# One fused attention and mixture-of-experts kernel, rewritten: stages ordered by a planner in the source, score blocks turned by VectorE, shares multiplied in by GpSimd, two experts per sum matmul

## The chip, the core and the metric

The kernel runs on one NeuronCore of a Trainium2 chip. The metric is the device time of one execution in microseconds (us). Engines are named as in the profile: PE is TensorE (matmuls; PEld its weight loads), DVE is VectorE, ACT is ScalarE, POOL is GpSimd, SP is SyncE, which here only issues DMAs. Everything is float32, or float32r for the largest matmuls.

## What is computed

Three layers follow each other, without a round trip to memory between them:

```
# 1: attention through 32 memory slots; B=4, H=8, S=576, head 64
a = softmax(phi over s);  k_m = a^T k;  v_m = a^T v          # (b,h,32,64)
x = softmax(q k_m^T / 8) v_m                                 # (2304, 512)
# 2: four experts, every token through each, weighted by its shares p
x = sum_e p[:, e] * (relu(x @ w1[e]) @ w2[e])                # F = 1024
# 3: eight experts on 32 slots (4 each)
logits = x @ phi2                                            # (2304, 32)
slots  = softmax(logits over tokens)^T @ x
out    = softmax(logits over slots) @ [relu(slots_e @ v1[e]) @ v2[e]]
```

## The kernel before

Layer 2 is never multiplied out for all tokens. `logits` needs only `h @ (w2[e] @ phi2)`, so a small matrix M = w2·phi2 is made once (`m_stages`, chunks of 512 rows: PE transposes L471, matmuls L485, fold L495). `slots` needs only the sums over tokens of token weight × share × h, which are multiplied by w2 at the very end. Layer 1 is folded too: the attention weights A stay unmultiplied, and v_m is multiplied into w1 instead, chunk by chunk (`g_mult`, L384; `g_out` splits the result G into a high and a low float32r half, L394 and L395).

The tokens go through in five **units**: the whole batches 0, 1 and 2 (two ranges of 288 tokens each), then the two halves of batch 3. A unit has 8 chunks n (expert n // 2, half of its 1024 hidden columns) of 4 blocks. One **up** (`up`, L425 to L427) is one block for one range: six float32r matmuls of 128 by 288 (high by high, high by low, low by high, for two halves of the contraction) into a PSUM bank of the pool `psm` (2 banks). ACT takes it out with the relu into hT (L431); once both ranges are there, DVE transposes hT in 32 by 32 blocks into `hid` (L433), so that tokens lie on partitions. There are 256 ups. After each chunk `logits` (L448) multiplies hT by M.

After each expert `expert` transposes the logits (L526) and multiplies by the expert's shares and adds up, on POOL for experts 0 to 2 (L532 to L535). After a unit, `group` follows: `whole` (PE, L543) gathers the logits, `stats` takes a running maximum and the exponentials (L551 to L571), `weights` makes `we` = weight × share, one slice per expert, expert 0 on POOL and 1 to 3 on DVE (L585), and `sums` (L596) multiplies `we` into `hid`: per block of 32 tokens and expert, four matmuls of 32 by 32 by 256 columns, one per 32 partitions, into four banks.

The attention of batch b+1 is made between the ups of batch b: `kv_stages` (maxima, exponentials, k_m, v_m) and, per tile of 128 queries, `q_stages`: four transposes of q (L287), scores with queries on the partitions (L300), softmax on DVE and ACT (L305 to L320), two PE transposes of the result (L328) and the split into A's halves (L333, L334). Five tiles make a batch; the last has 64 queries.

All orders are written out by hand: each engine runs its instructions in the order in which the source emits them (`manual_schedule`), and `pump` emits one background item after each block of ups. All DMAs go through SP's queue in the source's order. At the end, 160 blocks of 256 KB of w2, v1 and v2 stream through whatever buffers have come free (`fill`, `fetch`, `done`), from the start of the last unit on but for six; at the very end `combine` (L969, copies L976 and L978) writes the output in two column halves through a pool of 5 buffers.

One float32 matmul appears as two instructions in the profile, one float32r matmul as one; a transpose is one.

Of the kernel before, what the change touches and what calls it, by code (L numbers as in the profile page):

```python
# [1 line left out]

# [13 lines left out]
@with_exitstack  # L16
def kernel(
    ctx: ExitStack,
    tc: tile.TileContext,
    q: bass.AP,  # L20
    k: bass.AP,
    v: bass.AP,
    phi: bass.AP,
    dprob: bass.AP,
    w1: bass.AP,
    w2: bass.AP,
    phi2: bass.AP,
    v1: bass.AP,
    v2: bass.AP,
    out: bass.AP,  # L30
):
# [4 lines left out]

    nc = tc.nc
# [4 lines left out]
    FH = 512  # L46
# [3 lines left out]

    const = ctx.enter_context(tc.tile_pool(name="const", bufs=1))
    att = ctx.enter_context(tc.tile_pool(name="att", bufs=1))
    pc = ctx.enter_context(tc.tile_pool(name="pc", bufs=1))
    hTp = ctx.enter_context(tc.tile_pool(name="hTp", bufs=5))
    rawp = ctx.enter_context(tc.tile_pool(name="rawp", bufs=2))
    gp = ctx.enter_context(tc.tile_pool(name="gp", bufs=2))
    bigp = ctx.enter_context(tc.tile_pool(name="bigp", bufs=5))
    psm = ctx.enter_context(tc.tile_pool(name="psm", bufs=2, space=bass.MemoryType.PSUM))
    psl = ctx.enter_context(tc.tile_pool(name="psl", bufs=2, space=bass.MemoryType.PSUM))
    psa = ctx.enter_context(tc.tile_pool(name="psa", bufs=4, space=bass.MemoryType.PSUM))  # L60

    def bank():
        return psa.tile([128, 512], F32, tag="at", name="at")

    def mbank():
        return psm.tile([128, 512], F32, tag="mm", name="mm")

    def big(shape, name, dt=F32):
        return bigp.tile(shape, dt, tag="big", name=name)

    ident = const.tile([128, 128], F32)
    si = const.tile([128, 32], F32)
    rr = const.tile([128, 4, 32], F32)
    r2 = const.tile([128, 4, 32], F32)
    ind = const.tile([128, 3], F32)
    phi2_sb = const.tile([128, 4, NSLOT], F32)
    dp = const.tile([128, 18, E], F32)
    dps = const.tile([128, 18], F32)
    pe = const.tile([128, B, NT, E], F32)
    ct = const.tile([128, S], F32)  # L80
    A = [const.tile([128, 2, 2, S], F32R, tag=f"A{n}", name=f"A{n}") for n in range(2)]
    kbd = [const.tile([128, 4, 2, NM], F32, name=f"kbd{n}") for n in range(2)]
    vb = [const.tile([128, 128], F32, name=f"vb{n}") for n in range(2)]
    M = const.tile([128, 4 * NCH, NSLOT], F32)
    srun = const.tile([128, 8, 4, 32], F32)
    mrun = const.tile([128, 1], F32)
    zrun = const.tile([128, 1], F32)


    ph_t, kv_t, q_t = {}, {}, {}  # L90


    def load_phi(b):

        t = att.tile([128, 36, NM], F32, tag="ph", name="ph")
        src = phi[b].rearrange("(i c) s m -> c i s m", c=2)
        for c in range(2):
            nc.sync.dma_start(
                out=t[:, 16 * c:16 * c + 16, :].rearrange("p (i r) m -> p i (r m)", i=4),
                in_=src[c, :, 0:512, :].rearrange("i (p r) m -> p i (r m)", r=4),  # L100
            )
        for c in range(2):
            nc.sync.dma_start(
                out=t[64 * c:64 * c + 64, 32:36, :],
                in_=src[c, :, 512:576, :].rearrange("i p m -> p i m"),
            )
        ph_t[b] = t

    def load_kv(b, w):

        src = (k, v)[w][b].rearrange("(i c) s d -> c i s d", c=2)
        if w == 0:
            kv_t[b, "t"] = att.tile([128, 2, 4, HD], F32, tag="kt", name="kt")
            kv_t[b] = big([128, 2, 2, 4, 4 * HD], "kv")
        for c in range(2):
            nc.sync.dma_start(
                out=kv_t[b, "t"][64 * c:64 * c + 64, w],
                in_=src[c, :, 512:576, :].rearrange("i p d -> p i d"),
            )
        for c in range(2):  # L120
            nc.sync.dma_start(
                out=kv_t[b][:, w, c],
                in_=src[c, :, 0:512, :].rearrange("i (p r) d -> p i (r d)", r=4),
            )

    def load_q(b, ti):

        t = att.tile([128, H, HD], F32, tag="q", bufs=2, name="q")
        if ti < 4:
            nc.sync.dma_start(  # L130
                out=t, in_=q[b, :, 0:512, :].rearrange("h (p r) d -> r p h d", r=4)[ti]
            )
# [225 lines left out]
    def load_w1(s):  # L358
# [708 lines left out]
```

## Time and profile before

| | |
|---|---|
| time, median of 3 runs | 687.84 us (687.55, 687.84, 690.6) |
| span of the profiled execution | 690.1 us |
| busy share of the span, PE / DVE / ACT / POOL | 83% / 45% / 29% / 5% |
| chain that ended last, share by engine | PE 55%, DVE 17%, DMA 11%, ACT 7%, issue 6% |
| DMA in total | 106.22 MB, mean 154 GB/s |

The time of the profiled execution is not marked; only the run of 690.6 us is longer than the span of 690.1 us, so it stands at 690.6, with 0.5 us around the span. A busy PE is not PE at its peak: matmuls are pipelined, and the clock that was granted to PE moved between 1.2 and 2.4 GHz. "PEclk" gives it as a share of 2.4 GHz, as a mean over a stretch.

### The profile page before, as it was taken

How to read it: one execution, taken by the hardware profiler on the slowest of the kernel's cores; microseconds unless marked ns; L12 is line 12 of the kernel's file. 1: busy time of each engine (PE TensorE's matmuls, PEld its weight loads, DVE VectorE, ACT ScalarE, POOL GpSimd, SP SyncE). 2: the span in 40 equal slices, each digit the busy share in tenths (PEclk: the TensorE clock that was granted, in tenths of full speed). 3: DMA queues.
4: the chain of work that ended last, by engine and by line, in shares of the span. 5: the costliest groups of instructions: out<-in, count | busy, mean ns of one | idle time of the engine just before them, and what ended most of it. 6: DMA issues, size and time to landing. Idle time of an engine off the chain costs nothing.

```text
span 690.1 us, 15584 instructions
## 1 busy us (share of the span) xinstructions
PE 571.0 (83%) x6750; PEld 396.3 (57%) x6750; DVE 310.0 (45%) x663; ACT 196.8 (29%) x478; POOL 35.3 (5%) x39
## 2 busy tenths in 40 slices
PE   7688988788868889797789898867896996897885
PEld 6566775566646667565556776644555884332232
DVE  5665444533360854645356466444445453121012
ACT  2334332333330434333123334311333141010012
POOL 0000001001010001010100101010010010000000
PEclk9989998899979999979899999989998898899995
DMA  8858431333110763113047241511310497899995
GB/s 203 288 151 256 163 108 53 123 123 123 62 62 4 211 175 101 62 62 123 3 126 202 77 144 47 169 63 63 120 65 0 159 331 261 277 376 350 347 337 188
DMA packets 96867, 106.22 MB, mean 154 GB/s; under 512 B 30752, under 2 KB 64032, under 8 KB 96800
## 3 DMA queue, kind: packets, MB, share of 16 engines
q1 hardware_dynamic: 96800, 105.24, 48.1%
q8 instruction: 53, 0.87, 0.5%
q14 instruction: 14, 0.11, 0.1%
HBM read 100.50 MB, written 4.72 MB: 152 GB/s over the span
## 4 chain that ended last, share of the span: by engine, by line
PE 55%; DVE 17%; DMA 11%; ACT 7%; issue 6%; SPq 2%; POOL 1%; ACTq 0%; DVEq 0%; POOLq 0%
PE mm L425 10%; PE at L596 9%; PE mm L427 8%; DMA v<-in_moe_w_dram 8%; PE mm L426 7%; PE lb L448 6%; PE at L384 4%; DVE g L395 3%; DVE h L433 3%; ACT hT L431 3%; PE at L495 1%; PE mm L882 1%; DMA out_dram<-ot 1%; PE at L471 1%; PE at L485 1%
## 5 line engine op out<-in xcount | busy, mean ns | idle before, releaser
L425 PE MATMUL mm<-A,g 128*128 128x288 f32 x512 | 174.7, 341 | 13.7 <-ACT hT L431 12.7
L431 ACT ACTIVATE hT<-mm 128x288 f32<-128x288 f32 x256 | 104.2, 412 | 264.6 <-PE mm L427 264.1
L433 DVE STREAM_TRANSPOSE h<-hT 128x576 f32<-128x576 f32 (+1 forms) x160 | 104.4, 654 | 156.0 <-ACT hT L431 155.5
L427 PE MATMUL mm<-A,g 128*128 128x288 f32 x512 | 158.3, 309 | 7.7 <-DVE g L395 7.3
L426 PE MATMUL mm<-A,g 128*128 128x288 f32 x512 | 157.0, 307 | 0.0
L425 PEld LDWEIGHTS mm<-A,g 128*128 128x128 f32 x512 | 101.8, 199 | 67.7 <-ACT hT L431 33.4
L427 PEld LDWEIGHTS mm<-A,g 128*128 128x128 f32 x512 | 101.9, 199 | 11.2 <-DVE g L395 10.5
L426 PEld LDWEIGHTS mm<-A,g 128*128 128x128 f32 x512 | 102.6, 200 | 0.4
L596 PE MATMUL at<-h,we 32*32 32x256 f32 x2304 | 60.0, 449 | 25.4 <-POOL we L585 15.4
L596 PEld LDWEIGHTS at<-h,we 32*32 32x32 f32 x2304 | 41.6, 112 | 43.2 <-POOL we L585 17.0
L395 DVE TENSOR_TENSOR g<-at,g 128x512 fp32r<-128x512 f32 x64 | 42.7, 670 | 9.4 <-ACT g L394 9.4
L448 PE MATMUL lb<-hT,M 128*32 128x288 f32 x512 | 45.2, 460 | 0.0
L1021 PE MATMUL mm<-v,hz 128*8 128x256 f32 x256 | 34.8, 380 | 6.4 <-DMA v<-in_moe_w_dram 3.5
L384 PE MATMUL at<-raw,vb 64*32 64x512 f32 x512 | 38.9, 627 | 0.1
L394 ACT CAST g<-at 128x512 fp32r<-128x512 f32 x64 | 37.2, 582 | 0.2 <-PE at L384 0.2
L605 DVE SCALAR_TENSOR_TENSOR srun<-srun,fo,at 128x256 f32<-128x256 f32 x16 | 6.6, 475 | 47.3 <-PE at L596 47.3
L976 DVE COPY ot<-at 128x512 f32<-128x512 f32 x8 | 5.4, 690 | 48.4 <-PE at L969 36.2
L1021 PEld LDWEIGHTS mm<-v,hz 128*8 128x8 f32 x256 | 8.6, 87 | 30.8 <-DMA v<-in_moe_w_dram 20.0
L300 PE MATMUL at<-kbd,qt 128*128 128x64 f32 (+1 forms) x160 | 19.3, 264 | 5.9 <-ACT qt L291 5.3
L311 ACT ACTIVATE ex<-ex 128x256 f32<-128x256 f32 (+1 forms) x20 | 8.3, 417 | 51.6 <-DVE ex L307 51.6
L300 PEld LDWEIGHTS at<-kbd,qt 128*128 128x128 f32 (+1 forms) x160 | 17.8, 180 | 8.0 <-ACT qt L291 6.9
L448 PEld LDWEIGHTS lb<-hT,M 128*32 128x32 f32 x512 | 13.7, 118 | 14.8 <-issue 8.8
(148 smaller groups left out, 522.6 us busy)
## 6 DMA issues: line engine op xcount, KB each, us to landing
v<-in_moe_w_dram SPq DMA_DIRECT2D x160, 256.0 KB, 5.8
raw<-in_moe_w_dram SPq DMA_DIRECT2D x32, 1024.0 KB, 5.1
w<-in_moe_w_dram SPq DMA_DIRECT2D x16, 512.0 KB, 6.2
kv<-in_k_dram SPq DMA_DIRECT2D x8, 512.0 KB, 5.0
kv<-in_v_dram SPq DMA_DIRECT2D x8, 512.0 KB, 5.9
out_dram<-ot SPq DMA_DIRECT2D x16, 256.0 KB, 2.9
q<-in_q_dram SPq DMA_DIRECT2D x12, 256.0 KB, 6.5
ph<-in_phi_dram SPq DMA_DIRECT2D x8, 256.0 KB, 5.6
```

The source lines that it names most:

```text
L300: nc.tensor.matmul(sc[0:n, :, j, :], st["qt"][:, j, 0:n], kbd[b % 2][:, j], start=True, stop=True)
L384: nc.tensor.matmul(ts[c][32 * i:32 * i + 32, :], vb[b % 2][64 * c:64 * c + 64, 32 * i:32 * i + 32], raw[s][64 * c:64 * c + 64, i, :], star ...
L394: nc.scalar.copy(out=hi, in_=t)
L395: nc.vector.tensor_tensor(out=lo, in0=t, in1=hi.bitcast(F32), op=ALU.subtract)
L425: nc.tensor.matmul(ps, gh, ah, start=(c == 0), stop=False)
L426: nc.tensor.matmul(ps, gh, al, start=False, stop=False)
L427: nc.tensor.matmul(ps, gl, ah, start=False, stop=(c == 1))
L431: nc.scalar.activation(out=t[:, o0 - base:o1 - base], in_=ps, func=ACTF.Relu)
L433: nc.vector.transpose(out=hid[u, n // 2][:, 4 * (n % 2) + fb], in_=t[:, 0:o1 - base])
L448: nc.tensor.matmul(lb[u, ki][32 * a:32 * a + 32, 0:o1 - o0], M[:, 4 * n + a, :], hT[u, n, a][:, o0 - base:o1 - base], start=(f == 0), stop ...
L596: nc.tensor.matmul(ts[p][32 * e:32 * e + 32, 0:256], st["we"][rows, tb, e], hid[u, e][rows, :, tb], start=(tb == 0), stop=(tb == nt - 1),)
L1021: nc.tensor.matmul(acc[32 * i:32 * i + 8, :], hz[:, eb, g * fp + f, i, :], use((2, dh, eb, fp, i))[:, n_ * f:n_ * f + n_], start=(k_ == 0 ...
```

## The change

The whole program is written anew around the same arithmetic and the same units, ups, chunks and blocks.

1. **Orders.** Each step is added to a `Plan` with its engine, a cost typed into the source, what it reads and writes, and a due time `at`, counted in ups. `order` lets the engines run against these costs, always takes the step that could begin first (the earliest due among equals), and emits the steps in that order. Buffers and PSUM banks with more than one possible place are given out by `Uses`, from the order of the due times. There are 3 banks for ups instead of 2.
2. **Scores** are computed with the 32 slots on the partitions, 8 matmuls of 32 by 128 columns per tile in place of 4 of 128 by 64; DVE turns them in 32 by 32 blocks, and turns the softmax back; the two PE transposes per tile are gone. POOL does three steps per tile: subtract the maximum, multiply by the inverse sum, and A's low half.
3. **Shares.** POOL multiplies each block of h by the expert's shares, after DVE's transpose: 96 instructions of 128 by 576 and 64 of 128 by 288. `we` and its products are gone; the sums take the token weights `dt` directly.
4. **Sums.** One matmul takes two experts: 576 of 32 by 32 by 512 columns in place of 1152 of 256.
5. **Logits** of both ranges go to one bank, so `expert` handles 128 by 288 in place of 128 by 576.
6. **M** for all 8 chunks is due in the first half of unit 0 (before: over all of it).
7. **Last weights**: 40 blocks of 1 MB at 18 places; 3 are due before the last unit, 9 within it, 6 right after it; the others as blocks are used up. The output passes through 3 buffers instead of 5.
8. The 29 idle matmuls (`warm`) that stood between the first steps are gone.

The core of the diff:

```
-        return [s0, s1, s1b, s2]
+        def score():
+            for i in range(4):
+                for c in range(2):
+                    nc.tensor.matmul(
+                        sc[32 * i:32 * i + 32, n * c:n * c + n],
+                        kb[b % 2][:, c, 32 * i:32 * i + 32], qt[:, i, 0:n], start=True, stop=True,
+                    )
+        def top():
+            nc.vector.transpose(out=X, in_=sc)
+            nc.vector.tensor_reduce(out=mx, in_=Xv, axis=AX.X, op=ALU.max)
+        add(POOL, pool(2 * n), lambda: nc.gpsimd.tensor_tensor(
+            out=Xv, in0=Xv, in1=mx.unsqueeze(2).to_broadcast(full), op=ALU.subtract,
+        ), r=[key("mxq", s)], w=[xk], at=at[1] + 0.2)
...
+        add(PE, 0.81, f, r=[wk(go, 2048)] + a_part(b, 0, o0, w) + a_part(b, 1, o0, w), w=[pk(bm)], at=at)
...
+        add(DVE, dve(width), lambda: nc.vector.transpose(out=h_of(u, e)[:, kx], in_=t), r=[wk(ho, width)], w=[hk],
+            at=at + 0.4)
+        share = pe[:, b, tb0:tb0 + nt, e:e + 1].to_broadcast([128, nt, 32])
+        add(POOL, pool(width), lambda: nc.gpsimd.tensor_tensor(
+            out=h_of(u, e)[:, kx], in0=h_of(u, e)[:, kx], in1=share, op=ALU.mult),
+            r=["pe"], w=[hk], at=min(at + 10, starts[u + 1] + 1.5))
...
-            for e in range(E):
-                (nc.gpsimd if e == 0 else nc.vector).tensor_tensor(
-                    out=we[:, :, e], in0=dt_, in1=share(e), op=ALU.mult
-                )
...
-                        nc.tensor.matmul(
-                            ts[p][32 * e:32 * e + 32, 0:256], st["we"][rows, tb, e],
-                            hid[u, e][rows, :, tb], start=(tb == 0), stop=(tb == nt - 1),
-                        )
+        def sums(tbs):
+            for tb in tbs:
+                for ep in range(2):
+                    c = 2 * (tb % 2) + ep
+                    for p in range(4):
+                        rows = slice(32 * p, 32 * p + 32)
+                        nc.tensor.matmul(
+                            bank[S0 + p][32 * c:32 * c + 32, :], dtv[rows, tb, :],
+                            h_pair(u, ep)[rows, :, :, tb, :], start=(tb < 2), stop=(tb >= nt - 2),
+                        )
+        for t0 in range(0, nt, 2):
+            tbs = range(t0, min(t0 + 2, nt))
+            add(PE, 0.43 * len(tbs) + 0.02, lambda tbs=tbs: sums(tbs), r=["dt"] + hks, w=sb, at=at[3])
...
+    homes = [(PH, z3 - 31), (PH + 2048, z3 - 31), (RAW + 2048, z3 - 5)]
+    homes += [(GP + 2048 * n, z3 + 4 * n + 5) for n in range(2)]
+    homes += [(R[2] + 2048 * n, z3 + 10.5) for n in range(2)]
+    homes += [(AT[0], z3 + 13)]
+    homes += [(R[3] + 2048 * n, z3 + 17 + 4 * n) for n in range(4)]
+    homes += [(RAW, z4 + 1), (AT[1], z4 + 1)] + [(R[0] + 2048 * n, z4 + 10.5) for n in range(4)]
...
+    def ot_of():
+        o = uses(*[HT + 576 * n for n in (3, 4, 5)])
+        return at_place(o, 512), wk(o, 512)
```

What this does to the orders, at three places. On PE, at the end of unit 0, the sums stood in one piece between ups of unit 1 (L425 to L427; `at` are PSUM banks, `h` the blocks of h):

```order
L425 MATMUL mm<-A_96,g 128x288
L426 MATMUL mm<-A_96,g 128x288
L427 MATMUL mm<-A_96,g 128x288
L596 MATMUL at<-h,we 32x256 x288
L425 MATMUL mm<-A_96,g 128x288
L426 MATMUL mm<-A_96,g 128x288
L427 MATMUL mm<-A_96,g 128x288
```

Now (L745 to L747 are an up, L951 the sums, `ps` the banks, `h_91` and `h_185` two stretches of h) they begin like this, with `dts` the token weights:

```order
L746 MATMUL ps_95<-A,g 128x288
L747 MATMUL ps_95<-A,g 128x288
L951 MATMUL ps_98<-h_91,dts 32x512
L951 MATMUL ps_99<-h_91,dts 32x512
L951 MATMUL ps_100<-h_91,dts 32x512
L951 MATMUL ps_101<-h_91,dts 32x512
L951 MATMUL ps_98<-h_185,dts 32x512
```

After 16 of them an up follows: they come in 9 pieces of 16 matmuls instead of one of 288, with an up between the first six.

On PE, for one chunk of M in unit 0, the matmul L485 stood right behind the last transposes (L471), and the fold (L495) right behind it:

```order
L425 MATMUL mm<-A_95,g 128x288
L426 MATMUL mm<-A_95,g 128x288
L427 MATMUL mm<-A_95,g 128x288
L471 MATMUL at<-ident,w_137 128x128 x4
L485 MATMUL at<-w_137,phi_sb 32x512 x4
L495 MATMUL at<-si,mp 128x32 x4
```

Now (L834 the matmul, L846 the fold):

```order
L745 MATMUL ps_96<-A,g 128x288
L746 MATMUL ps_96<-A,g 128x288
L747 MATMUL ps_96<-A,g 128x288
L834 MATMUL ps_98<-h_185,phi_sb 32x512 x4
L745 MATMUL ps_94<-A,g 128x288
L746 MATMUL ps_94<-A,g 128x288
L747 MATMUL ps_94<-A,g 128x288
L745 MATMUL ps_94<-A,g 128x288
L746 MATMUL ps_94<-A,g 128x288
L747 MATMUL ps_94<-A,g 128x288
L846 MATMUL ps_99<-si,ct 128x32 x4
```

The last transposes stand two ups ahead of the matmul, and one up stands between it and the fold.

On POOL, before, the whole work for a unit:

```order
L532 TENSOR_TENSOR acc<-lt,pe 128x576
L534 TENSOR_TENSOR lt<-lt,pe 128x576
L535 TENSOR_TENSOR acc<-acc,lt 128x576
L534 TENSOR_TENSOR lt<-lt,pe 128x576
L535 TENSOR_TENSOR acc<-acc,lt 128x576
L585 TENSOR_TENSOR we<-dt,pe 128x18x32
```

Now, a piece from within unit 0 (L763 the share into h, L613, L624 and L638 the three steps of a query tile):

```order
L613 TENSOR_TENSOR atts<-atts,small 128x256
L763 TENSOR_TENSOR h_185<-h_185,pe 128x576 x2
L624 TENSOR_TENSOR atts<-atts,small 128x256
L763 TENSOR_TENSOR h_185<-h_185,pe 128x576
L638 TENSOR_TENSOR A<-atts,A 128x2x128
```

Between a query tile's steps stand one or two share products in POOL's queue.

## Rows read from the trace of the kernel before

**Rows 1.** The page, busy time of each engine.

```profile
PE 571.0 (83%) x6750; PEld 396.3 (57%) x6750; DVE 310.0 (45%) x663; ACT 196.8 (29%) x478; POOL 35.3 (5%) x39
```

**Rows 2.** Stretches: length, busy per engine (instructions), granted clock, DMA share, GB/s.

```profile
35.20:191.20 156.00, 131.32 (x1164) 100.94 (x1163) 71.89 (x158) 55.01 (x128) 6.41 (x5) 0.92 0.40 129
191.20:319.00 127.80, 110.48 (x1467) 83.25 (x1467) 67.98 (x127) 41.84 (x106) 8.17 (x6) 0.92 0.34 99
319.00:574.80 255.80, 214.14 (x2948) 157.04 (x2948) 129.82 (x261) 77.05 (x194) 18.16 (x18) 0.93 0.36 116
574.80:592.10 17.30, 9.42 (x290) 6.18 (x290) 5.14 (x15) 1.21 (x4) 1.39 (x2) 0.78 0.66 209
592.10:671.00 78.90, 71.21 (x518) 23.77 (x518) 8.52 (x32) 6.34 (x12) 0.00 (x0) 0.96 1.07 356
671.00:690.10 19.10, 9.56 (x47) 4.58 (x46) 5.04 (x9) 5.36 (x12) 0.00 (x0) 0.56 0.59 190
```

**Rows 3.** Waits of PE over the span: total us, times, longest.

```profile
PE at L596 <- POOL we L585: 15.4, 5, 5.2
PE mm L425 <- ACT hT L431: 12.7, 11, 3.5
PE at L485 <- DVE w L477: 9.8, 8, 1.5
PE at L596 <- issue: 8.9, 10, 1.3
PE at L543 <- DVE acc L535: 8.3, 5, 2.3
PE at L495 <- ACT mp L490: 7.8, 8, 2.6
PE mm L427 <- DVE g L395: 7.3, 14, 2.7
```

**Rows 4.** Timeline of unit 2: start, us, engine, line, operation.

```profile
402.86 1.18 PE L448 MATMUL lb<-hT,M 128*32 128x288 f32 x16
403.96 0.19 PEld L425 LDWEIGHTS mm<-A,g 128*128 128x128 f32 x1 [0.47 <-issue]
404.93 1.10 PE L300 MATMUL at<-kbd,qt 128*128 128x64 f32 x8
405.87 0.61 PE L287 MATMUL at<-ident,q 128*128 128x128 f32 x4
406.31 0.38 PE L328 MATMUL at<-ident,ex 128*128 128x128 f32 x2
406.45 0.38 PE L425 MATMUL mm<-A,g 128*128 128x288 f32 x1
```

**Rows 5.** The page, the group of the sums.

```profile
L596 PE MATMUL at<-h,we 32*32 32x256 f32 x2304 | 60.0, 449 | 25.4 <-POOL we L585 15.4
```

**Rows 6.** Timeline of PE: part of the sums of unit 0.

```profile
213.56 2.74 PE L596 MATMUL at<-h,we 32*32 32x256 f32 x128 [0.57 <-issue]
```

**Rows 7.** Groups by shape: busy us, mean ns of one, idle before.

```profile
L534 POOL TENSOR_TENSOR lt<-lt,pe 128x576 f32<-128x576 f32 x6 | 7.2, 1193 | 194.4 <-DVE lt L526 194.4
L585 POOL TENSOR_TENSOR we<-dt,pe 128x576 f32<-128x576 f32 x3 | 5.2, 1737 | 102.4 <-DVE dt L577 102.4
L534 POOL TENSOR_TENSOR lt<-lt,pe 128x288 f32<-128x288 f32 x4 | 2.8, 690 | 39.2 <-DVE lt L526 39.2
L433 DVE STREAM_TRANSPOSE h<-hT 128x576 f32<-128x576 f32 x96 | 74.1, 774 | 111.0 <-ACT hT L431 110.6
```

**Rows 8.** Timeline of unit 1: a DVE transpose while POOL works.

```profile
297.54 1.42 POOL L535 TENSOR_TENSOR acc<-acc,lt 128x576 f32<-128x576 f32 x1
297.76 0.78 DVE L433 STREAM_TRANSPOSE h<-hT 128x576 f32<-128x576 f32 x1 [1.64 <-ACT hT L431]
```

**Rows 9.** Timeline of PE: the first up.

```profile
35.22 0.61 PE L425 MATMUL mm<-A,g 128*128 128x288 f32 x1
```

**Rows 10.** Timeline of PE: the last matmuls on a streamed block.

```profile
668.90 2.25 PE L1021 MATMUL mm<-v,hz 128*8 128x256 f32 x16
```

More of the change, by code (lines that the diff above doesn't have):

```diff
@@ L59 @@
[L59 to L72, printed above, removed]
@@ L503, in m_stages @@
-        return [load] + [flip(a) for a in range(4)] + [part, fold]
-    begun = [False]
-    def group(u):
+        add(PE, 0.95, fold, r=["mp", "cst"], w=[pk(b2)], at=ats[6])
+        add(DVE, 0.3, lambda: nc.vector.tensor_copy(
+            out=M[:, 4 * n:4 * n + 4], in_=bank[b2][:, 0:128].rearrange("p (a s) -> p a s", a=4),
+        ), r=[pk(b2)], w=[("M", n)], at=ats[6] + 0.1)
+    begun = [False]
+    cmx, csm = small_at(NT), small_at(NT)
+    nm, mg2, zg, fo = small_at(1), small_at(1), small_at(1), small_at(1)
@@ new lines, in back @@
+        def back():
+            nc.vector.transpose(out=dt, in_=lc)
+            if not first:
+                nc.vector.tensor_copy(out=mrun, in_=mg2)
+                nc.vector.scalar_tensor_tensor(
+                    out=zrun, in0=zrun, scalar=fo, in1=zg, op0=ALU.mult, op1=ALU.add,
+                )
+        add(DVE, dve(w) + (0 if first else 0.4), back, r=["lc", "fo", "zg", "nm"], w=["dt", "mrun", "zrun"],
+            at=at[2])
+        hks = [wk(h_at(u, e), 256 * nt) for e in range(E)]
@@ L635 @@
[L635 to L636 removed]
+            nc.vector.transpose(out=ct[rows, base:end], in_=lr[rows])
+        add(DVE, 3 * dve(w) + 0.5, row_norm, w=["lr", ("ct", b), "mp"], at=at[5])
+    loads = [("w", kk) for kk in range(8)]
+    loads += [(1, eb, nn, c) for eb in range(2) for nn in range(2) for c in range(4)]
     PARTS = ((0, 256), (256, 512))
[L638 to L641 removed]
@@ L848, with spread @@
-        lu, ln = last
-        logits(lu, ln)
-        groups[lu][0](ln // 2)
-        wb[0] = mbank()
-        fill(const, "A1", 4, again=False)
-        gl = groups[lu][1]
-        for f in gl[:4]:
-            f()
-        for _ in range(2):
-            fill(rawp, "raw", 4)
-        for _ in range(2):
-            fill(gp, "g", 4)
-        rest = gl[4:]
-        rz = pc.tile([128, 1], F32, tag="rz", name="rz")
+    add(DVE, 1.0, norm, r=["dp"], w=["dpn"], at=2)
+    def spread(x, bk):
+        nc.tensor.matmul(
+            bank[bk][:, 0:72], rr[32 * x:32 * x + 32].rearrange("p i s -> p (i s)"),
+            dp[32 * x:32 * x + 32].rearrange("p t e -> p (t e)"), start=True, stop=True,
+        )
@@ new lines, in program @@
+    nload = [0]
+    for u, (b, ranges) in enumerate(units):
+        if b + 1 < B:
+            attention(b + 1, starts[u])
+        for n in range(NCH):
+            s = b * NCH + n
+            for fb in range(4):
+                for ki in range(len(ranges)):
+                    up(u, n, fb, ki)
+            if u < NU - 1 and s + 1 < NG:
+                g_mult(s + 1, place(u, n, 1) + 0.1)
+            logits(u, n, place(u, n + 1) + (0.6 if n < NCH - 1 else 1.6))
+            if n % 2:
+                expert(u, n // 2, place(u, n + 1) + 1.7)
+        z = starts[u + 1]
+        group(u, [z + 2.4, z + 3, z + 4, z + 8.6, z + 14, z + 16])
```

1654 lines of the change are left out of this document (926 added, 728 removed).

## The prediction

> **What bounds it now.** I read the page first: PE is busy for 83% of the span, DVE for 45%, POOL for 5% [rows 1]. That names PE, but a busy PE may be slow or waiting inside its pipeline, so I cut the span where PE's kind of work changes and read each stretch [rows 2]. The first up starts at 35.2 us [rows 9]; the last group of sums ends at 592.1; the last streamed block is used up at 671 [rows 10]. That gives four parts.
>
> - Start, 0 to 35.2 us: loads and the first attention.
> - Main, 35.2 to 592.1, the first four rows of the stretches, 556.9 us: DMA moves 99 to 209 GB/s, DVE is busy for 274.8 us and POOL for 34.1, so PE is the bound. It is busy for 465.4 us, idle for 91.5, and the granted clock is 0.92 on average over the four rows: about 16% of the time at 1.2 GHz.
> - Stream, 592.1 to 671: 356 GB/s with all DMA engines busy. DMA is the bound.
> - End, 671 to 690.1: the last fold, eight products, copies, output.
>
> Main splits further. If the low clock is spread evenly, 8% of 465.4 = 37 us of the busy time is clock loss, and 428 us is work at full clock. The waits [rows 3] name 70 of the 91.5 idle us: the sums for POOL's `we`, the ups for a bank that ACT empties, the two steps of M, the sums' own issue gaps, `whole` for POOL's additions, the low half of G. So main is 428 work + 37 clock + 91.5 idle, and each idle us costs 37/91.5 = 0.4 us more through the clock, if the two go together. I assume that, because the two lowest clocks of the stretches, 0.78 and 0.56, stand where PE is idle for about half of the time.
>
> **Work on PE.** The 1536 matmuls of the ups do not change. *Sums:* at full clock 128 instructions took 2.74 us, 21.4 ns each [rows 6], so 2304 take 49.3 us; the page's 60.0 [rows 5] has low clock in it, which I count as clock. Now there are 1152, each with twice the columns. If an instruction costs what it does now, they take 24.7 us; if a column does, 49.3. Between them I go by the logits: 16 instructions of 288 columns, four at a time side by side, took 1.10 us with what follows (402.86 to 403.96 [rows 4]), 275 ns each on its quarter; for 512 columns 489 ns, and with sixteen side by side 30.6 ns each: 35.2 us. Term: −14 (−25 to 0). *Queries:* 8 score instructions took 0.94 us and the two transposes of the result 0.14 [rows 4]. The new 16 of 128 columns lie between 0.49 (the logits' 1.10 by columns) and 1.10 (by count); I take 0.60, nearer the columns, since they too run four side by side. That is −0.48 for each of the 15 tiles in main: −7 (−9 to 0). *Cutting up the sums:* some 26 pieces between ups instead of 5. The weight load of the up behind a group of logits came 0.47 us late [rows 4], partly hidden; 21 more pieces cost 0 to 10, I take +5, half of the row. The Trainium skill (TensorEngine Tiling (Array Packing), Key Properties) says that changing the tiling mode drains the engine. By it both sides of each piece pay the 0.47, and the term is +20 and the time some 596 us; the row shows one side only. Work becomes 428 − 14 − 7 + 5 = 412.
>
> **Idle.** By the rows [rows 3], what I leave of each: sums for POOL's `we` 15.4 → 2: `we` is gone, and what the sums now need from POOL is the last share product, 0.69 to 1.19 us [rows 7], done while the exponentials run. Issue gaps 8.9 → 4: half the instructions. M 9.8 + 7.8 → 4: two ups stand before the matmul and one before the fold, and the waits were 1.2 and 1.0 us each, where an up takes some 0.97 (403.96 to 404.93 [rows 4]). Banks 12.7 → 3: a third bank. `whole` 8.3 → 3: other work fills it, except after the last unit. G 7.3 → 4. The unnamed 21 → 8: part of them waited on DVE for the two transposes that are gone. That leaves 28, with bounds of 0 and 91. POOL itself adds little: 96 × 1.19 + 64 × 0.69 = 159 us of share products [rows 7], about 27 for the three steps of 15 query tiles (0.63 us for 256 columns, on the line through these two rows) and some 18 for the logits, 204 us over a main of 450. DVE loses `we` and half of the logits' transposes and stays near 255. Both are covered by PE; if PE were to become shorter than 255, DVE would be late next. The clock loss falls with the idle time to 0.4 × 28 = 11. Main: 412 + 28 + 11 = 451, that is −106.
>
> *Moved:* M's 8.4 MB of w2 now have to arrive within the first half of unit 0, with 4 MB of w1 and 4 MB for batch 1's attention. Half of that unit is some 65 us, so 16.6 MB need 255 GB/s; the stream shows 356, so I cost it at nothing. At the 209 GB/s of main's fastest stretch it would be 79 us, 14 more.
>
> **The other parts.** *Start:* the first up needs three query tiles, not five, but v now loads ahead of q and the idle matmuls that kept PE going are gone: 35 → 31 (27 to 39). *Stream:* 78.9 us at 356 GB/s are 28.1 MB. Of the 40 blocks now, 14 can be in by the end of main, and 26 × 1.049 MB at that rate take 76.6; if only 12 are in, 82.5. I take 78. The 1 MB blocks are fewer issues on SP's queue, and stand there behind waits for freed places as the old ones did. *End:* 12 pieces of output of each half pass through 3 buffers, not 5, and PE stands behind the copies: 19 → 24 (19 to 31). Nothing else there changes.
>
> **Sum.** 31 + 451 + 78 + 24 = 584 for the span of 690.1. The profiled execution took 690.6, the median is 687.84, 2.8 less: **581 us**, and I say 580. By the unknown terms, work may lie 18 lower or 26 higher, idle with its clock 39 lower or 88 higher, the other parts 10 lower or 20 higher; not all at once: 520 to 640 for this case.
>
> **Rivals.** *PE nearly full.* The planner leaves PE no more than a few us of idle time, and what I called work holds pipeline tails in front of waits that go too. Idle 5, clock 2, work 380, start 28: 28 + 380 + 7 + 77 + 22 = 514, some 510 us. For it: DVE and POOL have room in every stretch. Against it: even the best stretch now, unit 1, is idle for 14%.
>
> *The stalls stay.* The order is fixed by costs typed into the source; if the chip hands over later than they say, each in-order queue waits where the plan did not. Idle stays 91 and clock 37: 412 + 128 = 540, in all 31 + 540 + 78 + 24 − 3 = 670 us. For it: every engine is strictly in order. Against it: most of the named waits lose their cause, not their place.
>
> *POOL in the way: slower.* A query tile now goes through POOL three times, and each step stands behind a share product. ACT and DVE wait for these steps in their own queues, and ACT empties the ups' banks. With 1.19 + 0.63 = 1.82 us per step, 45 steps in main and nothing hidden, PE idles 82 us more, times 1.4 for the clock: 580 + 115 = 695. With the price that POOL paid beside DVE, 1.74 for 1.19 [rows 7], the step is 2.66 and the time 748. It is slower than before from some 1.8 us per step on, with nothing hidden. Against it: three banks let PE run two ups ahead, 1.9 us. And a DVE transpose that ran while POOL worked took 0.78 us [rows 8], as its mean of 0.774, so the price of 1.74 holds for pairs like that of `we`, where DVE too takes two operands from SBUF. The Trainium skill (GPSIMD Engine Reference, Key points) says just that: contention comes with DVE instructions in a 2-port mode or with two SBUF inputs; the trace agrees, and by it 748 is out.
>
> *No change* would need the gains of main to be given back elsewhere, and no row has room for that.
>
> **Chances.** Forecast (520 to 640) 0.72; PE nearly full 0.06; stalls stay (640 to 684) 0.12; no change 0.02; slower 0.08. 520 to 655 holds the forecast and two thirds of the third case, 8 in 10. A measurement here tells 0.5% apart, 3.4 us: faster 0.90, same 0.02, slower 0.08.
>
> **What would show it.** Right: the sums' group near 35 us busy, with no wait for POOL above 2; a main of 430 to 480 us with PEclk of 0.96 or more; POOL busy for 200 us or more, share products at 1.2 us; DVE's transposes still at 0.77; the stream at 350 GB/s for 75 to 85 us; copies of the output waiting for out DMAs. Wrong: waits of ACT for POOL at L613's readers that add up to tens of us, PE waits for ACT's bank above 13, PEclk still at 0.92, or share products near 1.7 us.

## The result, and the profile after

The changed kernel took **566.2 us** (median of 4 runs, 564.62 to 566.57), the kernel before 689.22 us beside it (median of 4, 687.55 to 691.25): a ratio of 0.820, 95% interval 0.816 to 0.824. The forecast was 580, with a range of 520 to 655. The profiled execution took 566.41 us, 1.8 more than its span of 564.6. The page and the stretches, cut at the same places as [rows 2] (length, busy time of PE, PEld, DVE, ACT, POOL with instructions, granted clock, DMA share, GB/s); the last three rows are main as a whole, the stream, and the end:

```profile
PE 494.2 (88%) x5684; PEld 338.3 (60%) x5684; DVE 302.0 (53%) x609; ACT 204.7 (36%) x478; POOL 211.6 (37%) x252
```

```profile
37.60:164.00 126.40, 125.23 (x1267) 97.49 (x1269) 81.45 (x157) 62.38 (x143) 56.55 (x62) 0.99 0.53 159
164.00:278.00 114.00, 111.20 (x1562) 77.58 (x1554) 75.86 (x132) 47.68 (x115) 56.82 (x58) 1.00 0.36 112
278.00:455.00 177.00, 168.27 (x1986) 118.91 (x1977) 112.95 (x230) 73.22 (x177) 91.20 (x118) 0.97 0.52 171
...
37.60:458.45 420.85, 405.39 (x4802) 293.98 (x4800) 272.98 (x522) 183.28 (x435) 204.57 (x237) 0.98 0.48 151
458.45:533.00 74.55, 48.68 (x446) 20.35 (x450) 3.63 (x20) 4.67 (x8) 0.00 (x0) 0.79 1.07 353
533.00:564.60 31.60, 20.46 (x146) 9.20 (x140) 7.02 (x12) 6.79 (x14) 0.00 (x0) 0.75 0.53 168
```

| us | before | forecast | after |
|---|---|---|---|
| start, to the first up | 35.2 | 31 | 37.6 |
| main | 556.9 | 451 | 420.9 |
| of it: PE idle | 91.5 | 28 | 15.5 |
| of it: busy, clock loss and work | 465.4 | 423 | 405.4 |
| stream | 78.9 | 78 | 74.6 |
| end | 19.1 | 24 | 31.6 |

(The two columns at the sides cut stream and end at different places. Before, and in the forecast, the stream ends when the last streamed block is used up; after, it is cut where the last load has landed, at 533, with four blocks of v2 still to be used. Cut where PE's last wait for a load ends, at 667.4, the kernel before has 75.3 and 22.7; cut by the last block used, at 548.6, the kernel after has 90.1 and 16.0. Stream and end together need no cut: 98.0 before, 102 forecast, 106.2 after.)

The whole gain is in main. Some waits of PE over the span, beside [rows 3] (engine, tile and line, what it waited for: total us, times, longest):

```profile
PE ps L1309 <- DMA h<-in_moe_w_dram: 20.7, 2, 20.2
PE ps L445 <- DMA atts<-in_phi_dram: 10.3, 1, 10.3
PE ps L817 <- DVE g L683: 5.2, 1, 5.2
PE ps L495 <- ACT atts L477: 4.3, 3, 1.4
PE ps L1261 <- ACT hts L1272: 3.7, 2, 2.6
PE ps L951 <- DVE dts L933: 3.2, 1, 3.2
```

Of the waits of [rows 3] little is left: those for `we`, for ACT's banks, for the two steps of M, for the low half of G and the issue gaps do not appear (its high half has 0.8 us), and `whole` has 2.2. The 20.7 is v2 that has not arrived, in the stream; the 10.3 and 5.2 lie before the first up, as does a part of the 4.3; L1261 is the end. In main the largest wait is 3.2 us, once, after the last unit (L951: the sums, for `dt`). No wait there is for POOL. The groups that took over POOL's and DVE's part of the shares, and the sums (line, engine, operation, shape, count; busy us, mean ns of one; idle before):

```profile
L763 POOL TENSOR_TENSOR h<-h,pe 128x576 f32<-128x576 f32 x96 | 114.1, 1195 | 137.3 <-DVE h L759 98.2 <-DVE pe L1096 26.9 <-PE ps L747 7.4
L763 POOL TENSOR_TENSOR h<-h,pe 128x288 f32<-128x288 f32 x64 | 44.0, 702 | 43.9 <-DVE h L759 42.4 <-issue 0.5
```

```profile
L759 DVE STREAM_TRANSPOSE h<-hts 128x576 f32<-128x576 f32 x96 | 73.7, 770 | 39.8 <-ACT hts L753 39.2
```

```profile
L951 PE MATMUL ps<-h,dts 32*32 32x512 f32 x1152 | 43.7, 633 | 3.2 <-DVE dts L933 3.2
```

POOL pays its undisturbed price, 1195 ns [rows 7], and so do DVE's transposes beside it, 770 ns. Theory after this look: main is now PE's work and little else, because every in-order queue finds its input ready; that comes from the planned order rather than from any one part. Rivals: it comes from the parts (shares on POOL, a third bank, fewer sums), or POOL holds main up as it is. Start and end are accidents of a load's key and of three buffers.

### The profile page after: what moved, and what is told of

Read it like the earlier page. It is cut to its first block, busy times and chain, and to the rows that moved or that the text cites. A ratio compares the mean times of both kernels' runs of the same rounds, so it can differ in the third digit from the quotient of the medians.

```text
span 564.6 us, 13458 instructions
## 1 busy us (share of the span) xinstructions
PE 494.2 (88%) x5684; PEld 338.3 (60%) x5684; DVE 302.0 (53%) x609; ACT 204.7 (36%) x478; POOL 211.6 (37%) x252
## 4 chain that ended last, share of the span: by engine, by line
PE 81%; DMA 6%; DVE 5%; SPq 5%; ACT 1%; issue 1%; DVEq 0%; ACTq 0%
PE ps L745 15%; PE ps L747 12%; PE ps L746 12%; PE ps L951 7%; PE ps L672 6%; SPq L349 5%; PE ps L781 4%; PE ps L817 3%; PE ps L1214 3%; PE ps L788 2%; PE ps L1309 2%; PE ps L584 2%; PE ps L596 2%; DMA out_dram<-hts 2%; PE ps L495 2%; DMA h<-in_moe_w_dram 2%
## 5 line engine op out<-in xcount | busy, mean ns | idle before, releaser
L763 POOL TENSOR_TENSOR h<-h,pe 128x576 f32<-128x576 f32 (+1 forms) x160 | 158.0, 998 | 181.3 <-DVE h L759 140.6
L745 PE MATMUL ps<-A,g 128*128 128x288 f32 x512 | 163.3, 319 | 0.8 <-ACT g L681 0.8
L753 ACT ACTIVATE hts<-ps 128x288 f32<-128x288 f32 x256 | 105.7, 413 | 140.2 <-PE ps L747 138.7
L747 PE MATMUL ps<-A,g 128*128 128x288 f32 x512 | 152.0, 297 | 0.0
L746 PE MATMUL ps<-A,g 128*128 128x288 f32 x512 | 151.9, 297 | 0.0
L759 DVE STREAM_TRANSPOSE h<-hts 128x576 f32<-128x576 f32 (+1 forms) x160 | 102.9, 650 | 59.6 <-ACT hts L753 58.9
L745 PEld LDWEIGHTS ps<-A,g 128*128 128x128 f32 x512 | 96.8, 189 | 47.7 <-issue 25.1
L746 PEld LDWEIGHTS ps<-A,g 128*128 128x128 f32 x512 | 97.1, 190 | 0.1
L747 PEld LDWEIGHTS ps<-A,g 128*128 128x128 f32 x512 | 96.9, 189 | 0.3 <-DVE g L683 0.3
L683 DVE TENSOR_TENSOR g<-ps,g 128x512 fp32r<-128x512 f32 x64 | 41.0, 682 | 20.0 <-ACT g L681 20.0
L681 ACT CAST g<-ps 128x512 fp32r<-128x512 f32 x64 | 34.5, 590 | 44.7 <-PE ps L672 44.7
L951 PE MATMUL ps<-h,dts 32*32 32x512 f32 x1152 | 43.7, 633 | 3.2 <-DVE dts L933 3.2
L672 PE MATMUL ps<-raw,vb 64*32 64x512 f32 x512 | 37.7, 603 | 2.4 <-DVE srun L964 1.6
L1270 DVE COPY hts<-ps 128x512 f32<-128x512 f32 x8 | 5.3, 689 | 52.8 <-PE ps L1261 43.6
L781 PE MATMUL ps<-hts,M 128*32 128x288 f32 x384 | 28.3, 412 | 0.0
L951 PEld LDWEIGHTS ps<-h,dts 32*32 32x32 f32 x1152 | 15.7, 106 | 16.4 <-issue 13.4
L1309 PE MATMUL ps<-h,hts 128*8 128x256 f32 x80 | 6.2, 410 | 20.7 <-DMA h<-in_moe_w_dram 20.7
L613 POOL TENSOR_TENSOR atts<-atts,small 128x256 f32<-128x256 f32 (+1 forms) x20 | 11.5, 575 | 33.3 <-DVE small L611 33.1
L964 DVE SCALAR_TENSOR_TENSOR srun<-srun,small,ps 128x512 f32<-128x512 f32 x16 | 10.9, 743 | 18.4 <-PE ps L951 18.4
```

What stands on the lines that cost most here:

```text
L672: nc.tensor.matmul(bank[bs[c]][32 * i:32 * i + 32, :], vb[b % 2][64 * c:64 * c + 64, 32 * i:32 * i + 32], t()[64 * c:64 * c + 64, i, :], s ...
L681: add(ACT, act(512), lambda c=c, src=src: nc.scalar.copy(out=g()[:, 2 * c], in_=src), r=[pk(bs[c])], w=[wk(o + 1024 * c, 512)], at=at + 0.1)
L683: add(DVE, dve(512), lambda c=c, src=src: nc.vector.tensor_tensor(out=g()[:, 2 * c + 1], in0=src, in1=g()[:, 2 * c].bitcast(F32), op=ALU.s ...
L745: nc.tensor.matmul(t, gh, ah, start=(c == 0), stop=False)
L746: nc.tensor.matmul(t, gh, al, start=False, stop=False)
L747: nc.tensor.matmul(t, gl, ah, start=False, stop=(c == 1))
```

## Experiments

The ratio behind each is to the kernel before, run beside it on the same chip; the changed kernel's is 0.820.

**1. The shares on DVE.**

```
-        add(POOL, pool(width), lambda: nc.gpsimd.tensor_tensor(
+        add(DVE, dve(width), lambda: nc.vector.tensor_tensor(
             out=h_of(u, e)[:, kx], in0=h_of(u, e)[:, kx], in1=share, op=ALU.mult),
```

> The 160 share products move from POOL to DVE and nothing else is edited; the planner sets a new order with DVE's typed costs. DVE's products of this shape took 0.75 us in the kernel before (L585 on DVE, median 751 ns), so 96 of 0.75 and 64 of 0.45 us add 101 us to DVE's 273 of the 421 us between the first up and the last sums: 374, 89% of it. Theory (POOL takes work for which DVE's in-order queue has no room): PE waits for DVE's splits and transposes, main grows by 10 to 40 us, 576 to 606 us in all. Rival (POOL is in the way, ACT and DVE lose time waiting for its steps): main shrinks, 560 us or less. If DVE simply has room: 566, no change.

Measured: 571.99 us, ratio 0.829 (0.823 to 0.835): the interval overlaps the changed kernel's. By groups on DVE:

```profile
L763 DVE TENSOR_TENSOR h<-h,pe 128x576 f32<-128x576 f32 x96 | 73.8, 786 | 0.4
```

DVE was busy for 349.6 us of a main of 424.7, and PE's largest wait there for DVE was 4.9 us. So some 6 us, 3.9 of them in main, less than the theory's 10 to 40: DVE had room for nearly all of it, and handing the shares to POOL is not where the 123 us come from.

The two engines do meet, though not in the transposes. The product L874 reads two operands from SBUF and stands on POOL for three experts and on DVE for one; here it is in the changed kernel (first two lines), where POOL makes the shares, and in this run (last two), where DVE does:

```profile
L874 POOL TENSOR_TENSOR lts<-lts,pe 128x288 f32<-128x288 f32 x15 | 10.4, 690 | 1.7 <-DVE lts L871 1.5
L874 DVE TENSOR_TENSOR lts<-lts,pe 128x288 f32<-128x288 f32 x5 | 3.9, 773 | 0.1
...
L874 POOL TENSOR_TENSOR lts<-lts,pe 128x288 f32<-128x288 f32 x15 | 13.6, 904 | 200.8 <-DVE lts L871 200.8
L874 DVE TENSOR_TENSOR lts<-lts,pe 128x288 f32<-128x288 f32 x5 | 2.2, 443 | 0.0
```

DVE's product took 773 ns beside POOL's shares and 443 without them; POOL's took 690 ns, and 904 beside DVE's shares.

**2. POOL's share products doubled.**

```
+            nc.gpsimd.tensor_tensor(out=hb, in0=hb, in1=ones[:, 0:nt].to_broadcast([128, nt, 32]), op=ALU.mult)
```

> Each share product is followed by a second POOL product of the same shape, by a table of ones; the typed cost and so the order stay as they were. POOL's share products go from 158 to some 316 us, POOL in all from 205 to 363 of main's 421. Theory (POOL is covered by PE): 566 to 580 us. Rival (POOL is in the way: what follows a share product in POOL's queue is waited for by ACT and DVE): a good part of the 158 us appears, 610 to 695 us, and the waits of ACT and DVE for POOL grow from 3 us to tens.

Measured: 595.13 us, ratio 0.862 (0.855 to 0.870). Main, then a wait of ACT and one of DVE over the span:

```profile
33.60:493.90 460.30, 417.57 (x4803) 300.57 (x4801) 272.86 (x522) 179.05 (x435) 358.32 (x397) 0.96 0.43 139
```

```profile
ACT atts L617 <- POOL atts L614: 30.6, 14, 3.8
```

```profile
DVE atts L631 <- POOL atts L625: 23.2, 11, 3.8
```

Of 154 us more on POOL 29 appear, a time between what the theory and the rival said. Main is 39.5 us longer; stream and end are 6.5 shorter, and the first up came 4.0 earlier, for a reason that run 5 shows. The rival's mechanism is real: query steps stand behind share products, ACT waits 30.6 us for them, and the ups' banks come late (PE waited 12.7 us for ACT's relu). In the changed kernel ACT's wait for the same step is 3.1 us: POOL at 205 us of 421 is covered, at 358 of 460 it is not.

**3 and 4. One expert per matmul in the sums, in two orders.** First the two matmuls of a pair of experts directly behind each other, into two halves of the same rows:

```
-                            bank[S0 + p][32 * c:32 * c + 32, :], dtv[rows, tb, :],
-                            h_pair(u, ep)[rows, :, :, tb, :], start=(tb < 2), stop=(tb >= nt - 2),
+                            bank[S0 + p][32 * c:32 * c + 32, 256 * e2:256 * e2 + 256], dtv[rows, tb, :],
+                            h_pair(u, ep)[rows, e2, :, tb, :],
```

> The sums go back to one expert, 256 columns, per matmul: 2304 instructions instead of 1152, the same stages and typed costs, so the same order. Now the 1152 take 43.7 us. By the forecast's term (14 us from the smaller number of instructions): 580 us. If the columns alone set the time: 566 to 568 us. By the kernel before (2304 at 21.4 ns, 49.3 us at full clock): about 572 us.

Measured: 603.7 us, ratio 0.872 (0.862 to 0.881), 37 us more than the changed kernel, far above all three. The sums' own row in main (PE and PEld alone):

```profile
35.20:490.20 455.00, 80.32 (x2304) 58.66 (x2304) 0.99 0.44 143
```

34.9 ns per instruction, where the kernel before took 21.4 at full clock [rows 6] for the same shape. The edit had also changed which matmuls are neighbours: two in a row with the same weights into the same 32 by 32 part of the array. So a second form, in which sixteen in a row go to sixteen different parts, as before:

```
+                for e in range(E):
+                    x = 256 * (tb % 2)
+                    for p in range(4):
+                            bank[S0 + p][32 * e:32 * e + 32, x:x + 256], dtv[rows, tb, :],
```

> The sums again with one expert, 256 columns, per matmul, but now sixteen matmuls in a row go to sixteen different quarters by quarters of the array, as in the kernel before; each block of 32 tokens of odd number goes into the upper half of its bank's columns, so the sums come out in another place than the steps behind read them from. Stages, typed costs and order as in the changed kernel. Theory (a matmul holds its part of the array for its whole duration, 371 ns for 256 columns and 587 ns for 512, and 16 work side by side; the run with one expert per matmul was slow, 80.3 us of sums, since its two matmuls in a row shared a part): 2304 / 16 x 371 ns = 53.4 us of sums, 10 us more than now, 574 to 578 us. Rival (the number of instructions sets the time, some 35 ns each): 80 us again, 597 to 607 us.

Measured: 580.24 us, ratio 0.844 (0.839 to 0.850). The sums, and a wait that is new:

```profile
37.60:471.90 434.30, 53.44 (x2304) 32.14 (x2304) 0.98 0.46 147
```

```profile
PE ps L951 <- issue: 4.0, 4, 1.3
```

53.4 us as the theory said, in total. Piece by piece it does not hold: an undisturbed piece of 64 took 22.3 ns per instruction (166.01 to 167.44), and the changed kernel's pieces take 33.4 (run 5), where the theory has 23.2 and 36.7. The totals are higher because they hold slow stretches, such as the last unit's sums in the changed kernel, at 54 ns each:

```profile
447.94 7.75 PE L951 MATMUL ps<-h,dts 32*32 32x512 f32 x144 [3.20 <-DVE dts L933]
```

With 9.7 us more of sums and 4.0 of issue gaps, one matmul for two experts is worth **14.0 us** of the time. The forecast had 14 for the sums alone and 4.9 for the gaps.

**5. The sums in one piece.**

```
-        for t0 in range(0, nt, 2):
-            tbs = range(t0, min(t0 + 2, nt))
+        for t0 in range(0, nt, nt):
+            tbs = range(nt)
```

> The sums of a unit stand in one stage instead of five (or, in the last two units, five of half the length), so no up stands between them; otherwise as it was. By the forecast's term for cutting them up (5 us, 0 to 10): 561 us. By the rule of the Trainium skill (TensorEngine Tiling (Array Packing), Key Properties) that each change of the tiling mode drains the engine, with the row's 0.47 us at both sides of each piece: some 546 us. Rival (the ups in between are what covers the waits of the other engines, which find PE's banks and h free later): 570 us or more.

Measured: 556.86 us, ratio 0.808 (0.802 to 0.815): **9 us less**, 7.9 of them in main, so cutting the sums up was a loss. The timeline of PE at unit 0's sums, in the changed kernel (start, us, line), and here:

```profile
165.31 0.29 PE L745 MATMUL ps<-A,g 128*128 128x288 f32 x1
165.71 0.29 PE L745 MATMUL ps<-A,g 128*128 128x288 f32 x1
166.19 1.14 PE L951 MATMUL ps<-h,dts 32*32 32x512 f32 x32
167.26 0.40 PE L745 MATMUL ps<-A,g 128*128 128x288 f32 x1
167.77 0.30 PE L745 MATMUL ps<-A,g 128*128 128x288 f32 x1
168.26 1.14 PE L951 MATMUL ps<-h,dts 32*32 32x512 f32 x32
```

```profile
164.82 9.74 PE L951 MATMUL ps<-h,dts 32*32 32x512 f32 x288
```

An up has two L745, 0.40 us apart, so it takes some 0.80; between two pieces it took 1.00 (167.26 to 168.26). The 32 instructions of a piece took 1.07 to the next start, 33.4 ns each; in one piece they take 33.6 (164.82 to 174.50). So a change from 128 by 128 to 32 by 32 matmuls and back costs 0.20 us. The trace of the changed kernel has 22 pieces, since some stages stand side by side, and here there are 5; of the 17 breaks that are gone 13 held an up, which is 2.6 us (the other four held a group of logits). Main fell by 7.9 us: 3.0 of busy time, and 5.0 of idle time, nearly all in two waits of PE, L672 for the banks that the sums hold (2.4 before the edit, none here) and L495 for ACT (2.9 and 0.6).

The first up came 2.4 us earlier too, though PE has the same order up to there. PE's first step, the second 32 matmuls of v_m and the first up, in the changed kernel and here:

```profile
10.31 0.45 PE L445 MATMUL ps<-ident,atts 128*128 128x128 f32 x1 [10.31 <-DMA atts<-in_phi_dram]
23.48 1.08 PE L495 MATMUL ps<-h,atts 128*32 128x64 f32 x32
37.60 0.59 PE L745 MATMUL ps<-A,g 128*128 128x288 f32 x1
```

```profile
11.30 0.45 PE L445 MATMUL ps<-ident,atts 128*128 128x128 f32 x1 [11.30 <-DMA atts<-in_phi_dram]
22.96 0.65 PE L495 MATMUL ps<-h,atts 128*32 128x64 f32 x32
35.16 0.59 PE L745 MATMUL ps<-A,g 128*128 128x288 f32 x1
```

PE began 1.0 us later here and was ahead at v_m, because it went faster: 0.65 us instead of 1.08 for the same work. The other runs agree. From PE's first step to the first up it is 23.9 to 24.5 us where v_m took 0.65 (runs 2, 3, 5), 27.3 to 27.6 where v_m and the scores behind it were slow (the changed kernel, runs 1, 4, 6), and 25.8 where only v_m was (run 11). So 3 us of the start are the speed of PE, and it differs from run to run: among the seven runs in which nothing ahead of it was edited the first up came between 35.2 and 38.0 us.

**6. Two banks for the ups.**

```
-        bm = mm()
+        bm = uses(*MM[:2])
```

> Ups get two PSUM banks instead of three, as in the kernel before; the planner orders anew. By the forecast (a third bank takes 9.7 of the 12.7 us that ups waited for ACT to empty a bank, times 1.4 for the clock): 580 us, with the wait of PE for ACT's banks back at 10 us or more. Rival (the order alone hides ACT, a bank more or less is nothing): 564 to 569 us.

Measured: 568.47 us, ratio 0.820 (0.814 to 0.826): no difference. PE's waits list no wait for ACT's relu. The term of 9.7 us for the third bank falls; with the planned order two banks hide ACT as well.

**7. The order of the due times.** The planner's simulation is left out.

```
-        return [stages[n][4] for _, n in out]
+        return [s[4] for s in stages]
```

> The planner's simulation is left out: every engine runs its stages in the order of the due times, as typed. Stages, banks, splits and due times stay. Theory (the order that the planner finds against its costs is what took PE's idle time from 91 us to 16): idle back to 60 to 120 us, the granted clock of main down from 0.98 to 0.93 or less, 640 to 720 us. Rival (the due times already interleave the work, the planner only ties knots): 566 to 585 us.

Measured: 638.05 us, ratio 0.920 (0.914 to 0.927). Main, and the longest waits of PE up to its end:

```profile
44.80:528.60 483.80, 428.87 (x4804) 315.88 (x4804) 260.95 (x512) 174.88 (x434) 200.98 (x235) 0.95 0.42 133
```

```profile
PE ps L744 <- ACT g L680: 11.4, 1, 11.4
PE ps L744 <- ACT hts L752: 7.7, 7, 1.6
PE ps L595 <- ACT atts L587: 6.3, 6, 1.2
PE ps L833 <- DVE g L682: 6.1, 4, 2.1
```

Main is 63 us longer, the start 7, stream and end 4. The edit sets the order of every queue anew, the DMA queue's too. The 11.4 lies before the first up. Main's idle time is 54.9 us, spread over fifteen kinds of wait, none above 8 us: the stalls that a rival of the forecast foretold, and just below what the theory said. With 72 of the 123 us the planner's order, over all queues together, is the largest single cause that was found. It is not all: without it the kernel is still 51 us faster than before, and of the 76 us of idle time that main lost only 39 come back. Which parts, or which typed due times, keep the other 37 away no run separates; `we`, the costliest wait of [rows 3], was never put back.

**8 to 10. The start, and nine places for the output.** The tails of phi, k and v get keys of their own; with 68 idle transposes on PE; and this with nine output buffers:

```
-                32768, w=[("ph", 2)], at=at,
+                32768, w=[("ph", 2 + c)], at=at,
...
+    warm(50, [], -199)
```

> The two tails of phi (and of k and v) get keys of their own, so that the planner does not hold the second back until the first has landed. Theory (the start was late because PE's first step waited until 10.3 us for the fourth load of phi, issued at 5.05): it is issued by 3.2 us, PE begins some 3 us earlier, the first up comes at 33 to 36 instead of 37.6, 562 to 564 us. Rival (the chain of DVE's query steps or PE's clock sets the first up, the tail had slack): 565 to 567 us.

> As the run with keys of their own for the tails, and 68 idle 128 by 128 transposes on PE: 50 before its first step, 8 and 10 behind the first two. Theory (the start is run by a PE at half speed: 32 matmuls of k_m take 1.08 us where the kernel before took 0.65): those take 0.65 us, k_m and the scores come 3 to 5 us earlier, the first up at 28 to 32, 557 to 561 us. Rival (DMA and DVE set the first up): no faster than the run with the tails alone.

> The tails' keys, the idle transposes at the start and nine places for the output together. If the terms add: 566 less 6 for the start and 7 for the end, 550 to 556 us. If the end is set by DMA alone: as the run with the idle transposes, 557 to 561 us.

Measured: 582.74 us (ratio 0.843, 0.836 to 0.850), 588.73 (0.849, 0.843 to 0.855) and 577.25 (0.836, 0.829 to 0.842), all slower than the changed kernel. The edit was incomplete: some readers of the tail kept the old key alone, so the plan loads the next batch's second tail ahead of them. They wait for it, once in each batch but the last, and take the last 64 rows of phi for half of the heads from the next batch; the time includes these waits:

```profile
PE ps L500 <- DMA atts<-in_phi_dram: 19.3, 3, 12.4
PE ps L445 <- DMA atts<-in_phi_dram: 5.0, 1, 5.0
```

So the totals say nothing on the start. Two rows ahead of that wait do: PE's first step now waits until 5.0 us, not 10.3 (run 8, as the lines above), and with the idle transposes (run 9) the 32 matmuls of k_m take 0.65 us as in the kernel before, not 1.08.

**11. Nine places for the output alone.**

```
-        o = uses(*[HT + 576 * n for n in (3, 4, 5)])
+        o = uses(*[HT + 576 * n for n in (3, 4, 5, 1, 2)], *[R[2] + 512 * n for n in range(4)])
```

> Nine places for pieces of the output instead of three; the planner orders anew. Theory (the end is long because the last v2 blocks stand on PE behind combines whose copies wait for output DMAs, 20 us of DVE's and ACT's waits): these waits go, the last v2 block is used by 541 instead of 547.5, the end shrinks from 31 to 22 to 26 us, 557 to 562 us. Rival (the output's 4.7 MB over the DMA engines set the end, 13.5 us at 350 GB/s behind the last load and the last combine): 564 to 567 us.

Measured: 555.73 us, ratio 0.805 (0.800 to 0.810): **10 us less**, 7.4 of them in stream and end. The stream and the end of this run, to compare with the last two rows of the stretches above:

```profile
454.20:529.00 74.80, 50.02 (x446) 21.71 (x450) 3.62 (x20) 4.67 (x8) 0.00 (x0) 0.75 1.06 347
529.00:553.00 24.00, 13.82 (x146) 6.78 (x142) 6.83 (x12) 6.66 (x14) 0.00 (x0) 0.80 0.74 237
```

The end is 24.0 us instead of 31.6, cut where the last load has landed; no copy waits for an output DMA (before the edit ACT's L1272 did for 10.9 us, DVE's L1270 for 9.2). Stream and main are as long as they were within 3 us.

**12. All that helped**, with the tails' keys completed: sums in one piece, nine places, the tails, 48 idle transposes.

> The sums of a unit in one piece, nine places for the output, keys of their own for the tails (now also in the list of what the later steps read), and 48 idle transposes on PE before and between the first steps. By the two runs that did the first two of these alone, 9.3 and 10.5 us; with a start as the run with the idle transposes showed it until its wait (32 matmuls of k_m in 0.65 us, PE's first step at 5.3 us instead of 10.3) the first up comes at 28 to 32 instead of 35 to 38, 4 to 7 us: 538 to 544 us. Rival (DMA sets the time from the last unit on, so what main and start give is waited for in the stream): 546 to 553 us.

Measured: **543.25 us** (541.95 to 543.95), ratio 0.790 (0.786 to 0.794), against 0.820: faster than both kernels. Main 408.6, stream and end 98.6 us. The start fell short: the first up came at 34.6 us, not 28 to 32. Timeline of PE there:

```profile
5.68 0.42 PE L445 MATMUL ps<-ident,atts 128*128 128x128 f32 x1
9.50 0.65 PE L500 MATMUL ps<-h,atts 128*32 128x64 f32 x32 [0.46 <-ACT atts L482]
15.41 0.66 PE L597 MATMUL ps<-ident,h 128*128 128x128 f32 x4 [1.38 <-DMA h<-in_q_dram]
17.61 1.11 PE L597 MATMUL ps<-ident,h 128*128 128x128 f32 x4 [1.44 <-DMA h<-in_q_dram]
18.65 1.08 PE L500 MATMUL ps<-h,atts 128*32 128x64 f32 x32
34.56 0.61 PE L758 MATMUL ps<-A,g 128*128 128x288 f32 x1
```

Now PE waits for q, which loads behind k and v, and after these gaps it is at the low speed again (the same 32 matmuls in 0.65, then in 1.08). The 3 us that the start gained on the changed kernel are no more than its spread from run to run (run 2, with the old key, had its first up at 33.6), so what the load and the transposes are worth stays open.

## Why the prediction was right, and where its steps were not

The time lies 14 us below the forecast; the sign and the bound are as forecast, and the gain is idle time and what the clock loses with it. That the total came so close is partly luck: main came out 30 us below its 451 (15 less work, 12 less idle time, 3 less clock loss), and start, stream and end 11 us above their 133. Of the engines POOL was counted right (204 us, 204.6 measured). DVE was not: 273.0 us in main instead of near 255, since the count left out what moved to POOL, the turning of the scores, and that some of DVE's steps take longer beside POOL. PE covered it. By the steps:

- **Idle, 28 left.** 15.5 was left. The steps that failed are four of the remainders: banks 3, M 4, G 4 and issue gaps 4 were forecast and less than 1 us was measured; the sums' wait, `whole` and the unnamed part came out near their 13. The reason given, that most waits lose their cause, is right in part only. The third bank was not needed (run 6), and the shares could stay on DVE (run 1). Of the 76 us of idle time that went, 39 come back without the planner's order (run 7), because each in-order queue then meets inputs that are not ready; the other 37 stay away, and why each of them does was not tested. The rival "the stalls stay" was therefore the nearest danger, and at 638 us it would still have been a gain of 8%.
- **0.4 us of clock for each idle us.** An assumption from two stretches. Busy time × (1 − granted clock) over idle time is 37.2 / 91.5 before, 21.4 / 54.9 without the planner, 16.7 / 42.7 with POOL doubled, 8.1 / 15.5 after, 4.0 / 10.5 in the last run: 0.41, 0.39, 0.39, 0.52, 0.38. The clocks are read to two digits, so the three with much idle time bear it out and the last two are too loose to.
- **Work, 412.** 405.4 × 0.98 is 397. The sums' term, −14, was mis-sized: at full clock an instruction takes 33.4 ns, not 30.6, so 1152 take 38.5 us and the term is −11 by the forecast's own 49.3; against run 4 it is −9.7. (The 43.7 of the row holds the slow stretches.) The queries: L300 and L328 were busy for 21.0 us in main, L596 now for 9.3, −11.7 where −7 was forecast (clock included). Groups on PE overlap each other, so the rest, some 10 us, cannot be given to single lines.
- **Cutting up the sums, +5 (0 to 10).** 22 pieces, not 26; 0.20 us for each break with an up, 3 us of busy time; with the idle time that it brings, main gains 7.9 in run 5. The Trainium skill (TensorEngine Tiling (Array Packing), Key Properties) says that a change of mode drains the engine. The timeline agrees that there is a price, and it is 0.20 us for both sides of a piece; +20 us, from 0.47 on each side, was more than four times too much.
- **POOL in the way.** Did not decide. The reason given was three banks, and two do as well (run 6). Run 2 shows the place from which it does: at 358 us of POOL main grows by 39 us and the time by 29. That DVE's transposes do not pay was weighed rightly: 770 ns beside a POOL that is busy for half of main. The Trainium skill (GPSIMD Engine Reference, Key points) lets DVE's instructions with two SBUF inputs contend; run 1 agrees, with L874 at 690 and 904 ns on POOL, 773 and 443 on DVE.
- **Moved M, nothing.** Right: the stretch from 37.6 to 164 us moved 159 GB/s and PE was idle for 1.2 us in it.
- **Start, 31.** Failed, by 6.6 us and in sign against before. The step: "the first up needs three query tiles, not five" was taken as worth more than the idle matmuls. What the runs show is the speed of PE: without the idle matmuls it went through k_m, in the changed kernel v_m and the scores too, at the low speed (1.08 against 0.65 us), and from v_m on that is worth some 3 us (run 5). The forecast also overlooked that the planner holds a load back behind another with the same key, so PE's first step waited until 10.3 us (5.0 without that, run 8); what this costs stays open, since run 12 without it began its first up at 34.6.
- **End, 24 (19 to 31), and stream, 78.** 106.2 together, 4 more than forecast. The step "three buffers, not five" had the right cause: with nine places the two shrink by 7.4 (run 11). But its place was wrong: PE stands behind the copies with the last four blocks of v2, which the forecast had in the stream. By the forecast's own cut the stream took 90.1 us and the end 16.0. The loads themselves came as forecast, at 353 GB/s.

## What to carry to other kernels

Where several waits of a few us each, for different engines, add up to a seventh of the span, look at the order before the parts: one order that lets every queue find its input was worth 72 us here, while the number of banks or the engine of a product was worth 0 to 6. Look too at what such a planner does with loads that share a key, and price small things at the two ends of the program from their own rows, since little covers them there: six more output places were worth 7 us in stream and end, and the speed of PE 3 us in the start. Do not cut a run of small matmuls into pieces only to mix it with large ones.

## What the runs showed of the hardware that was not expected

- The same 2304 matmuls of 32 by 32 by 256 took 53.4 us when sixteen neighbours in the order used sixteen parts of the array, and 80.3 us when two neighbours shared one (runs 4 and 3): the order of the matmuls alone costs half as much again.
- A POOL product of 128 by 576 took 1195 ns, the same on DVE 786: a factor of 1.5. A product with two operands in SBUF on either engine took longer while the other one made the shares (run 1), DVE's transposes did not.
- In the start of the changed kernel the 32 matmuls of k_m took 1.08 us instead of 0.65, while the stretch in which they lie reads a granted clock of 1.00 (the third figure from the end; columns as above):

```profile
14.50:20.00 5.50, 5.50 (x94) 4.82 (x94) 2.00 (x3) 1.92 (x4) 0.00 (x0) 1.00 1.18 285
```

There the durations have to be read, not the clock. (In run 12 the stretch from 17.6 to 24.8 us, with the same work at 1.08, reads 0.58.)
